# Query features of tiles 4 to 7 transposed as float32, straight from the buffer in which VectorE made them

## The chip, the cores and the metric

The kernel runs on one core of one Trainium2 chip. The metric is device time of one execution in microseconds; the time before is the median of three runs, 615.56 us (614.28 to 615.72). One further execution was recorded by the hardware profiler, and all times of single instructions come from that one.

## The reference

A block works on 2048 tokens of 512 features. The input is normalized; the result is the input plus two branches, a linear attention with learned softmax features and a gated MLP with a mixing over the tokens.

```python
# xn = layernorm(x); result: x + A(xn) + B(xn)
# branch A, 32 heads of 16
pq  = einsum("bhsd,hdf->bhsf", q, w_phi)          # pk in the same way
phi_q = concat([softmax(pq), softmax(-pq)], -1)   # 32 features per head
kv  = einsum("bhsf,bhsd->bhfd", phi_k, v);  z = sum of phi_k over the tokens
o   = (phi_q @ kv) / (phi_q . z + 1e-6);    A = o @ wo
# branch B, 688 channels
z1, z2 = split(gelu(xn @ w_in));  z2 = layernorm(z2)
B = (z1 * (w_sp @ z2 + b_sp)) @ w_out
```

## The kernel before, in words

**Tiles and number forms.** The tokens are 16 tiles of 128. Large products are done in float32r with each operand split into a rounded part h and a rest l: `mm3` (lines 57 to 59) adds ah·bh, ah·bl and al·bh. ScalarE rounds (`round_h`, line 49), VectorE subtracts (`rest_l`, line 53).

**Stages.** First the projections q, k, v and the sums over the keys; then the MLP's input product; then the product with `w_sp` (lines 887 to 930), written as seven products per pair of token tiles; last the stage that the change is in (from line 934): for each pair of tiles i, i+1 it adds up `u @ w_out` (`project_u`, TensorE lines 57 to 59 and 1030), applies `kv` to the query features (`attend`, line 1016), and adds `o @ wo` (`project_o`), whose result goes to `out` by an accumulating DMA on POOL's queue (line 1049).

**Query features.** The exponentials of the queries were stored to DRAM in an early stage (`e_d`). In the last stage `load_q(s, slot("et"))` (line 557) brings tile s back on SP's queue, five tiles ahead. `q_fin` (lines 564 to 571) makes the finished features on VectorE: the product with `zb` into a scratch `tmp` (564), sums and reciprocals (565 to 569), and the scaling in place in `et` (571). `attend` needs them transposed, tokens along the free dimension. There are three ways:
- tiles 0, 1 and 8 to 15 are transposed in blocks of 32 by VectorE (`turn_q`, line 580), put in order by four DMAs to DRAM (`q_d`, line 582), and loaded back (line 958 for tiles 8 to 15);
- tiles 2 and 3 are transposed by TensorE as float32 with `ident` (line 999);
- tiles 4 to 7 are copied by a DMA on POOL's queue from `et` into a float32r tile `er` (line 964) and transposed by TensorE with a float32r identity `ident_r` (line 1001), which ScalarE rounded behind `zb` (line 916).

For a pair, 16 transposes of 128x128 go to four PSUM tiles; ScalarE copies them out (line 1003), and `attend` reads the copies.

**Buffers and order.** `et`, the scratch `tmp`, `zb`, `c` and the weights `wu` share the pool `xz`, 16 buffers of the same size (`slot`). A buffer is free when the last instruction that uses its tile is done; whoever gets it next waits for that. `er` and the tiles `ft` of 8 to 15 come from another pool of three buffers (`er_pair`). The instructions of an engine are put in order by a planner that simulates the program; `tc.issue_after(ins)` orders what a block writes on the engine of `ins` behind `ins`, and only that. `lasts` and `fin` hold such instructions. `lasts[6]` is the last copy into `er`, on POOL; at `i == 2` the load of `z1` for the last gate (line 787, POOL) is put behind it (lines 1103 to 1105).

Of the kernel before, what the change touches and what calls it, by code (L numbers as in the profile page):

```python
# [10 lines left out]
F32 = mybir.dt.float32  # L11
F32R = mybir.dt.float32r
# [6 lines left out]
P = 128  # L19
# [5 lines left out]
NF = 2 * D  # L25
# [16 lines left out]
def mixer(ctx: ExitStack, tc: tile.TileContext, x, x_t, wv, wqkT, phi_bd, wo, w_in, wst, b_r, w_out, out):  # L42
    nc = tc.nc
    pe, act, dve, pool, sp = nc.tensor, nc.scalar, nc.vector, nc.gpsimd, nc.sync


    def round_h(eng, h, src):
        if eng is act:
            return act.activation(h, src, AF.Copy).ins  # L49
        return eng.tensor_copy(h, src).ins  # L50
# [21 lines left out]
    def xz_tile(n, dt, name):  # L72
        return xz.tile([P, SL], dt, tag="xz", name=name)[:, :n]
# [12 lines left out]
    ident = cst.tile([P, P], F32, name="ident")  # L86
# [17 lines left out]
    def group(e, j):  # L104

        return e[:, j * P:(j + 1) * P]
# [88 lines left out]
    with ExitStack() as p0:  # L195
# [154 lines left out]
        def proj_k(s):  # L350
            er = (spare[s] or stage("er")).rearrange("p a b -> p (a b)")[:, :NF + 2 * H] if s in spare else None
            return softmax_pair(wk, proj(s, wqk_h[:, 1], wqk_l[:, 1]), "k", r_x[:, s:s + 1], er=er)
# [69 lines left out]
        def turned(s):  # L422
            pt, i = transposed(s)
            keep(pe=i)
            return pt
# [15 lines left out]
        for cs, pt in zip(halves, pts):  # L441
            src = pt.rearrange("p a b -> p (a b)")
# [11 lines left out]
        pt = turned(1)  # L454
# [26 lines left out]
        pt = turned(2)  # L481
# [24 lines left out]
        for s in range(NT):  # L506
# [6 lines left out]
            er = ek[s] if s < len(ek) else proj_k(s)  # L513
# [42 lines left out]
    def load_q(s, et):  # L556
        sp.dma_start(et[:, :NF + 2 * H], e_d[s])
        return et

    def q_fin(et, tmp, zb):  # L560

        e, r, t, w = et[:, :NF], *(et[:, NF + k * 2 * H:NF + (k + 1) * 2 * H] for k in range(3))
        den = et[:, NF + 6 * H:QW]
        dve.tensor_tensor(tmp, e, zb, op=ALU.mult)
        dve.tensor_reduce(t, heads(tmp), axis=AX.X, op=ALU.add)
        dve.tensor_tensor(t, t, r, op=ALU.mult)
        dve.scalar_tensor_tensor(den, pairs(t, 0), EPS_DEN, pairs(t, 1), op0=ALU.add, op1=ALU.add)
        dve.reciprocal(den, den)
        dve.tensor_tensor(w.rearrange("p (h a) -> p h a", a=2), r.rearrange("p (h a) -> p h a", a=2),
                          den.unsqueeze(2).to_broadcast([P, H, 2]), op=ALU.mult)  # L570
        return e, dve.tensor_tensor(heads(e), heads(e), bc(w, 2 * H), op=ALU.mult).ins
# [25 lines left out]
    def load_a(n):  # L597
        i, q = SEQ[n]
        f = []
        for k in range(2):  # L600
            t = ws.tile([P, QC, P], F32, tag=f"f{k}", bufs=2, name="wf")
            sp.dma_start(t, wst[2 * i + k, :, q * QC:(q + 1) * QC, :])
            f.append(t.rearrange("p (k two) t -> p two k t", two=2))
        return f
# [27 lines left out]
    with ExitStack() as p1:  # L632
        tmp1 = p1.enter_context(left("tmp1", 1))
        kvT = tmp1.tile([P, D], F32, name="kvT")
        zb = tmp1.tile([P, NF], F32, name="zb")
# [41 lines left out]
        for s in range(NE):  # L677
            et = load_q(s, tb.tile([P, QW], F32, name="et") if s else tmp1.tile([P, 4, D], F32, tag="zhl", name="et").rearrange("p a b -> p (a b)")[:, :QW])
            tmp = zw.tile([P, 4, FC], F32, tag="z2", bufs=2, name="qtmp").rearrange("p a b -> p (a b)")[:, :NF]
            e, _ = q_fin(et, tmp, zb)  # L680
# [57 lines left out]
    for s in range(NT):  # L738
# [8 lines left out]
        for k, q in p:  # L747
            ins = act.activation(z[(slice(None), *k)], q, AF.Gelu_apprx_tanh, scale=r_x[:, s:s + 1]).ins
# [35 lines left out]
    def load_z1(i):  # L784
        t = gt.tile([P, 2, FH + REM], F32, tag="z1", name="z1t")
        for k in range(2):
            pool.dma_start(t[:, k, :FH], z1_d[2 * i + k])  # L787
        return t

    def products(n, g):  # L790
        i, q = SEQ[n]
        ops = A.pop(n)
        for name, an, bn in FORM:
            if n % NQ == 0:
                g[name] = psg.tile([P, D], F32, tag="g", name="g")
            dst = g[name][:, :FC]
            for k in range(2):
                (ah, al), (bh, bl) = ops[an], B[2 * q + k][bn]
                mm3(dst, (ah[:, k], al[:, k]), (bh, bl), n % NQ == 0 and k == 0, n % NQ == NQ - 1 and k == 1)
# [44 lines left out]
    def slot(name, dt=F32):  # L844
        return xz_tile(2 * FH, dt, name)
# [22 lines left out]
    def first_gate(i):  # L868
        n = KF * P
        a, b = xz_tile(2 * n, F32R, "u_uh"), xz_tile(n + P, F32R, "ul_rt")  # L870
        u = load_u(i, a[:, :n].bitcast(F32), b[:2 * REM, n:n + P])
        return split_u(*u, k_tiles(a[:, n:2 * n]), k_tiles(b[:, :n]))

    lasts, wu = [None] * 9, []
# [8 lines left out]
            load_w(w_out, rows, h, l, t[c // 2][:, c % 2 * D:(c % 2 + 1) * D])  # L883
            wu.append((h, l))

    g, es, ets, ft, ep, brought = {}, {}, {}, {}, {}, {}
    for n in range(NC):
        i = SEQ[n][0]
        if n % NQ == 1 and i < NP - 1:
            z = load_z1(i)  # L890
        products(n, g)
        if n % NQ == NQ - 1 and i < NP - 1:
            c = gt.tile([P, 2, FU], F32, tag="c", name="c")
            cq = c[:, :, :FH].rearrange("p k (j f) -> p k j f", j=2)
            cb = drain(i, g, cq)
            g = {}
        if n + 3 < NC:
            raw[n + 3] = load_a(n + 3)
        if n + 2 < NC:
            A[n + 2] = prep_a(n + 2, raw.pop(n + 2))  # L900
        if n % NQ == NQ - 1 and i < NP - 1:
            turn = gate(i, cb, z, c, z, prep_a.last)
            if i < NP - 2:
                turn()
            if i in (2, 4):
                s = i // 2 - 1
                e, t = (gt.tile([P, 2, FU], F32, tag=tag, name=name).rearrange("p k f -> p (k f)")[:, :NF]
                        for tag, name in (("c", "c"), ("z1", "z1t")))
                pool.dma_start(e, e_d[s, :, :NF])
                turn_q(s, t, e, pool)  # L910
        if n == NC - 4:
            stage_w()
        if n == NC - 3:
            zs = slot("zb", F32R)
            zb, ident_r = zs[:, :NF].bitcast(F32), zs[:, NF:NF + P]
            round_h(act, ident_r, ident)
            sp.dma_start(zb, zb_d)
            uT = [first_gate(0)]
            ets[2] = load_q(2, slot("et"))
            es[2], last = q_fin(ets.pop(2), slot("qtmp")[:, :NF], zb)  # L920
        if n == NC - 2:
            fq = [slot("f")[:, :NF].rearrange("p (k b c t) -> p k b c t", k=2, c=NB // 2, t=BL) for h in range(2)]
            for k in range(2):
                for h in range(2):
                    sp.dma_start(fq[h][:, k], q_d[k].rearrange("p (b h w) -> h p b w", h=2, w=QB // 2)[h])
            t = xz_tile((KF + 1) * P, F32R, "u1")
            us = {1: load_u(1, t[:, :KF * P].bitcast(F32), t[:2 * REM, KF * P:(KF + 1) * P])}
# [8 lines left out]
    cw = ctx.enter_context(left("cw", 1))  # L936
# [5 lines left out]
                      cw.tile([2 * REM, P], F32R, tag="rt", bufs=6, name="rt"))  # L942

    def er_pair(name):
        return cw.tile([P, 2, NF], F32R, tag="er", bufs=3, name=name)

    def features(s):
        with tc.issue_after(fin[-1]):
            tmp = slot("qtmp")[:, :NF]
            es[s], ins = q_fin(ets.pop(s), tmp, zb)  # L950
        fin.append(ins)
        if s == 3:
            return
        if s >= TQ:
            if s % 2 == 0:
                ft[s] = er_pair("f").bitcast(F32)
            turn_q(s, tmp, es.pop(s), pool)
            brought[s] = sp.dma_start(ft[s - s % 2][:, s % 2], q_d[s]).ins
            return
        e = es[s]  # L960
        if s % 2 == 0:
            ep[s] = er_pair("er")
        es[s] = ep[s - s % 2][:, s % 2]
        lasts[6] = pool.dma_start(es[s].bitcast(F32), e).ins

    def gated(u):
        return split_u(*u, wk.tile([P, KF, P], F32R, tag="uh", name="uh"), wk.tile([P, KF, P], F32R, tag="ul", name="ul"))
# [16 lines left out]
    def attend_T(s):  # L984

        if not s:
            t = [f.rearrange("p k b c t -> p (k b) c t") for f in fq]
            return [t[g // 2][:, :, g % 2 * 2:g % 2 * 2 + 2].rearrange("p b c t -> p c b t") for g in range(NG)]
        if s in ft:
            t = ft[s].rearrange("p k (b c t) -> p (k b) c t", c=NF // P, t=BL)  # L990
            return [t[:, :, 2 * g:2 * g + 2].rearrange("p b c t -> p c b t") for g in range(NG)]
        fs = []
        for g in range(NG):
            pt = pst.tile([P, 2, 2, P], F32, tag="tr", name="ptq")
            for a in range(2):
                for k in range(2):
                    src = group(es[s + k], 2 * g + a)
                    if src.dtype == F32:
                        pe.transpose(pt[:, a, k], src, ident)
                    else:  # L1000
                        pe.transpose(pt[:, a, k].bitcast(F32R), src, ident_r)
            f = wk.tile([P, 2, 2 * P], F32, tag="f", bufs=NG + 1, name="f")
            lasts[5] = act.activation(f, pt.rearrange("p a k b -> p a (k b)"), AF.Copy).ins
            fs.append(f)
        return fs
# [140 lines left out]
```

## Time and profile before

| | us |
|---|---|
| median of three runs (lowest, highest) | 615.56 (614.28, 615.72) |
| the profiled execution, its own time | 615.49 |
| its span in the profile | 613.7 |
| TensorE busy (share) | 606.0 (99%) |
| VectorE busy (share) | 518.8 (85%) |
| ScalarE busy (share) | 261.1 (43%) |
| POOL busy (share) | 134.7 (22%) |

Times in the trace are counted from the start of the span. PE is TensorE's matmul side and PEld its weight load, DVE is VectorE, ACT ScalarE, POOL GpSimd, SP the engine that only issues DMAs. A group is named by its line, its engine, the tile that it writes and the tiles that it reads. Matmuls are pipelined, so the distance from one start to the next tells what a group takes, and not the durations. A wait in brackets names what ended it. The last stage runs from about 480 us to the end.

### The profile page before, as it was taken

Reading aid. Unit: us, or ns where it says so; the run is one execution under the profiler, and the core shown is the slowest. Engines: PE = TensorE matmul, PEld = TensorE weight load, DVE = VectorE, ACT = ScalarE, POOL = GpSimd, SP = SyncE. Lnnn points to the kernel's source line nnn. Section 1 sums busy time; section 2 is a strip of 40 time slices with the busy share of each in tenths; the row PEclk is TensorE's granted clock in tenths of the full one; section 3 lists DMA queues with packets and bytes.
Section 4 is the critical chain, followed back from the end, with each engine's and each line's share of the span. In section 5 each row is a group of like instructions: output and inputs, shape, how many; then the busy total and the mean of one; then the engine's idle time right before and its main releaser. Section 6 shows DMA issues by size and latency. Waiting matters only on the chain.

```text
span 613.7 us, 11396 instructions
## 1 busy us (share of the span) xinstructions
PE 606.0 (99%) x4286; PEld 551.0 (90%) x4286; DVE 518.8 (85%) x929; ACT 261.1 (43%) x416; POOL 134.7 (22%) x236
## 2 busy tenths in 40 slices
PE   8999999999999999999999999999999999999996
PEld 6888888888888999999999999999999977777775
DVE  5999999999988578899889897877879999999921
ACT  4653324423433547887434443342345343332221
POOL 4122232333111014552000002000100042243520
PEclk9999999999999999999999999999999999999999
DMA  9557876566537849001454646455566799898882
GB/s 310 195 128 178 219 173 186 150 161 171 137 113 210 273 159 321 5 1 35 149 128 141 186 97 184 135 156 148 166 172 206 230 342 328 280 278 238 204 212 59
DMA packets 58414, 109.95 MB, mean 179 GB/s; under 512 B 12456, under 2 KB 24616, under 8 KB 58120
## 3 DMA queue, kind: packets, MB, share of 16 engines
q1 hardware_dynamic: 43400, 64.96, 34.9%
q0 software_dynamic: 12656, 38.64, 24.9%
q10 hardware_dynamic: 2304, 5.64, 2.4%
q8 instruction: 33, 0.54, 0.4%
q14 instruction: 21, 0.17, 0.1%
HBM read 66.85 MB, written 35.80 MB: 167 GB/s over the span
## 4 chain that ended last, share of the span: by engine, by line
PE 85%; DVE 6%; DMA 5%; issue 2%; SPq 1%; ACT 1%; POOL 0%; ACTq 0%; DVEq 0%; POOLq 0%
PE g L57 9%; PE g L58 9%; PE g L59 9%; PE proj L57 7%; PE proj L58 7%; PE proj L59 7%; PE zps L58 6%; PE zps L57 6%; PE zps L59 6%; PE pout L57 4%; PE pout L59 4%; PE pout L58 4%; DMA zacc<-e 1%; PE kvps L373 1%; PE po L1016 1%
## 5 line engine op out<-in xcount | busy, mean ns | idle before, releaser
L57 PE MATMUL g<-B,A 128*128 128x344 f32 x448 | 142.5, 319 | 0.4 <-DVE c L810 0.4
L58 PE MATMUL g<-B,A 128*128 128x344 f32 x448 | 142.3, 319 | 0.0
L59 PE MATMUL g<-B,A 128*128 128x344 f32 x448 | 138.9, 318 | 0.0
L57 PEld LDWEIGHTS g<-B,A 128*128 128x128 f32 x448 | 84.0, 188 | 1.0 <-DVE c L810 0.7
L58 PEld LDWEIGHTS g<-B,A 128*128 128x128 f32 x448 | 84.0, 188 | 0.0
L59 PEld LDWEIGHTS g<-B,A 128*128 128x128 f32 x448 | 83.6, 188 | 0.0
L49 ACT ACTIVATE A<-S 128x512 fp32r<-128x512 f32 x64 | 39.3, 628 | 71.2 <-DVE S L622 47.1
L57 PE MATMUL proj<-wqk_h,xT 128*128 128x512 f32 x128 | 50.1, 391 | 0.0
L59 PE MATMUL proj<-wqk_h,xT 128*128 128x512 f32 x128 | 49.8, 389 | 0.0
L58 PE MATMUL proj<-wqk_l,xT 128*128 128x512 f32 x128 | 49.8, 389 | 0.0
L125 ACT ACTIVATE e<-e,r_x 128x1024 f32<-128x1024 f32 x26 | 29.8, 1149 | 42.3 <-DVE e L124 41.3
L53 DVE TENSOR_TENSOR A<-S,A 128x512 fp32r<-128x512 f32 x64 | 43.0, 687 | 3.0 <-ACT A L49 2.8
L49 ACT ACTIVATE A<-wf 128x512 fp32r<-128x512 f32 (+1 forms) x64 | 32.8, 515 | 27.4 <-DMA wf<-in_wst 17.5
L57 PE MATMUL zps<-w1h,xT 128*128 128x344 f32 (+2 forms) x128 | 40.8, 320 | 0.0
L58 PE MATMUL zps<-w1l,xT 128*128 128x344 f32 (+2 forms) x128 | 40.7, 318 | 0.0
L59 PE MATMUL zps<-w1h,xT 128*128 128x344 f32 (+2 forms) x128 | 40.7, 318 | 0.0
L57 PE MATMUL zps<-w2h,xT 128*128 128x344 f32 (+2 forms) x128 | 40.7, 318 | 0.0
L58 PE MATMUL zps<-w2l,xT 128*128 128x344 f32 (+2 forms) x128 | 40.6, 317 | 0.0
L59 PE MATMUL zps<-w2h,xT 128*128 128x344 f32 (+2 forms) x128 | 40.3, 317 | 0.0
L53 DVE TENSOR_TENSOR A<-wf,A 128x512 fp32r<-128x512 f32 (+1 forms) x64 | 35.1, 553 | 3.9 <-ACT A L49 3.7
L128 DVE TENSOR_REDUCE sm<-e 128x64 f32<-128x1024 f32 x26 | 31.1, 1200 | 2.5 <-ACT e L125 2.5
L787 POOL DMA_DIRECT2D z1t<-z_d x16 | 8.7, 552 | 108.3 <-DMA wf<-in_wst 71.0
(222 smaller groups left out, 1437.4 us busy)
## 6 DMA issues: line engine op xcount, KB each, us to landing
wf<-in_wst SPq DMA_DIRECT2D x64, 256.0 KB, 3.4
e_d<-e POOLq DMA_DIRECT2D x16, 544.0 KB, 4.6
et<-e_d SPq DMA_DIRECT2D x16, 544.0 KB, 7.2
z_d<-z1f ACTq DMA_DIRECT2D x16, 344.0 KB, 3.1
z1t<-z_d POOLq DMA_DIRECT2D x16, 344.0 KB, 4.8
zacc<-e POOLq DMA_DIRECT2D x10, 512.0 KB, 4.8
u<-u_d SPq DMA_DIRECT2D x15, 320.0 KB, 5.8
xt<-in_x SPq DMA_DIRECT2D x16, 256.0 KB, 4.0
```

The source lines that it names most:

```text
L49: return act.activation(h, src, AF.Copy).ins
L53: return (eng or dve).tensor_tensor(l, src, h.bitcast(F32), op=ALU.subtract).ins
L57: pe.matmul(dst, ah, bh, start=start, stop=False)
L58: pe.matmul(dst, ah, bl, start=False, stop=False)
L59: return pe.matmul(dst, al, bh, start=False, stop=stop).ins
L125: softmax_pair.last = less, act.activation(e, e, AF.Exp, scale=scale).ins
L128: dve.tensor_reduce(sm, heads(e), axis=AX.X, op=ALU.add)
L373: i = pe.matmul(kv_acc[k:k + QP, m // 4], vs[:, m * QP:(m + 1) * QP], e[:, m * HP:(m + 1) * HP], start=first and m < 4 and len(ready) == n ...
L787: pool.dma_start(t[:, k, :FH], z1_d[2 * i + k])
L1016: lasts[3] = pe.matmul(po[r][c * QP:(c + 1) * QP, k], kvT[rows, m // 2, cols], fs[m // 4][rows, m // 2 % 2], start=True, stop=True).ins
```

## The change

The float32r copies of tiles 4 to 7 are gone: no `er` pair is taken for them and no DMA copies them. `features` returns after `q_fin`, and `attend_T` transposes all of tiles 2 to 7 from `et` as float32 with `ident`. The buffers in `et` are thus in use until TensorE has read them. The float32r identity and its rounding are gone, so `zb` is a plain float32 buffer. `lasts[6]` becomes the last VectorE instruction of `q_fin` (line 571) for the tiles 3 to 7. `er_pair` keeps its size and its three buffers and serves tiles 8 to 15 alone.

```diff
-    g, es, ets, ft, ep, brought = {}, {}, {}, {}, {}, {}
+    g, es, ets, ft, brought = {}, {}, {}, {}, {}
...
         if n == NC - 3:
-            zs = slot("zb", F32R)
-            zb, ident_r = zs[:, :NF].bitcast(F32), zs[:, NF:NF + P]
-            round_h(act, ident_r, ident)
+            zb = slot("zb")[:, :NF]
             sp.dma_start(zb, zb_d)
...
     def er_pair(name):
-        return cw.tile([P, 2, NF], F32R, tag="er", bufs=3, name=name)
+        return cw.tile([P, 2, NF], F32, tag="er", bufs=3, name=name)
 
     def features(s):
         with tc.issue_after(fin[-1]):
             tmp = slot("qtmp")[:, :NF]
             es[s], ins = q_fin(ets.pop(s), tmp, zb)
         fin.append(ins)
-        if s == 3:
-            return
         if s >= TQ:
             if s % 2 == 0:
-                ft[s] = er_pair("f").bitcast(F32)
+                ft[s] = er_pair("f")
             turn_q(s, tmp, es.pop(s), pool)
             brought[s] = sp.dma_start(ft[s - s % 2][:, s % 2], q_d[s]).ins
             return
-        e = es[s]
-        if s % 2 == 0:
-            ep[s] = er_pair("er")
-        es[s] = ep[s - s % 2][:, s % 2]
-        lasts[6] = pool.dma_start(es[s].bitcast(F32), e).ins
+        lasts[6] = ins
...
-                    src = group(es[s + k], 2 * g + a)
-                    if src.dtype == F32:
-                        pe.transpose(pt[:, a, k], src, ident)
-                    else:
-                        pe.transpose(pt[:, a, k].bitcast(F32R), src, ident_r)
+                    pe.transpose(pt[:, a, k], group(es[s + k], 2 * g + a), ident)
```

## The prediction

> **What bounds the kernel now.** I read the page first: span, busy shares, the slices and the chain that ended last.
>
> ```profile
> span 613.7 us, 11396 instructions
> ...
> PE 606.0 (99%) x4286; PEld 551.0 (90%) x4286; DVE 518.8 (85%) x929; ACT 261.1 (43%) x416; POOL 134.7 (22%) x236
> ...
> PE   8999999999999999999999999999999999999996
> ...
> PE 85%; DVE 6%; DMA 5%; issue 2%; SPq 1%; ACT 1%; POOL 0%; ACTq 0%; DVEq 0%; POOLq 0%
> ```
>
> TensorE is busy for 606.0 of 613.7 us and carries 85% of the chain. A saving elsewhere counts only where TensorE waits for it. So the next view is what TensorE waited for, from 20 us before the first instruction that the change touches (455 us) to the end:
>
> ```profile
> engine line waited for: us in total, times, longest us
> PE g L57 <- DVE c L810: 0.4, 1, 0.4
> PE ptq L1001 <- DMA er<-et: 0.2, 1, 0.2
> ```
>
> There are two waits in 159 us, and only one belongs to the code that changes: a transpose of L1001 waits 0.2 us for a copy `er<-et`. That is nearly all there is to win. What can be lost is TensorE time in the transposes themselves, and cover on the engines that feed it. The timeline of TensorE around the three groups of transposes (pairs 2/3, 4/5, 6/7) gives the prices; the columns are start, duration, and in brackets the idle time before it:
>
> ```profile
> 501.80 0.39 PE L59 MATMUL pout<-woh,oT 128*128 128x512 f32 x1
> 502.04 1.91 PE L999 MATMUL ptq<-ident,et 128*128 128x128 f32 x16
> 503.70 0.48 PE L57 MATMUL pout<-wu,uh 128*128 128x512 f32 x1
> ...
> 518.04 0.39 PE L59 MATMUL pout<-woh,oT 128*128 128x512 f32 x1
> 518.27 0.46 PE L1001 MATMUL ptq<-zb,er 128*128 128x128 f32 x4
> 518.97 1.23 PE L1001 MATMUL ptq<-zb,er 128*128 128x128 f32 x12 [0.24 <-DMA er<-et]
> 520.04 0.47 PE L57 MATMUL pout<-wu,uh 128*128 128x512 f32 x1
> ...
> 534.40 0.39 PE L59 MATMUL pout<-woh,oT 128*128 128x512 f32 x1
> 534.63 1.49 PE L1001 MATMUL ptq<-zb,er 128*128 128x128 f32 x16
> 535.96 0.47 PE L57 MATMUL pout<-wu,uh 128*128 128x512 f32 x1
> ```
>
> The kernel already holds both forms. Pair 2/3 goes the float32 way (L999), and its 16 transposes hold TensorE from 502.04 to 503.70, 1.66 us or 104 ns each. Pair 6/7 goes the float32r way with nothing to wait for: 534.63 to 535.96, 1.33 us or 83 ns each. Pair 4/5 takes 518.27 to 520.04, 1.77 us, which is the same work with the copy's wait in it (1.77 - 1.33 = 0.44 us lost, of which the bracket shows 0.24 as idle).
>
> **The change, part by part.** *Transposes.* 32 of them go from float32r to float32. Pair 4/5: from 1.77 to 1.66 us, since the wait goes too, -0.11. Pair 6/7: from 1.33 to 1.66, +0.33. TensorE is the path that sets the end, so the sum is +0.22 us. Bounds: if float32 cost no more than float32r, 2 x 1.33 against 1.77 + 1.33 is -0.44; if each transpose passed through the array four times, it would be spaced like a matmul of 512 columns, 0.23 us (518.04 to 518.27), 16 x 0.23 = 3.68 us a pair, +4.26. I take 1.66 because that row is the same operation on the same kind of tile.
>
> The weight loads of the two forms look alike:
>
> ```profile
> L999 PEld LDWEIGHTS ptq<-ident,et x16: 138/140/143, 501.8 to 503.6; 128*128 128x128 f32 x16
> L999 PE MATMUL ptq<-ident,et x16: 270/273/273, 502.0 to 503.7; 128*128 128x128 f32 x16
> ...
> L1001 PEld LDWEIGHTS ptq<-zb,er x32: 138/142/143, 518.0 to 535.8; 128*128 128x128 f32 x32
> ```
>
> The Trainium skill ("TensorE: Matmul & The Clock Gate", Weight-path perf modes) speaks against this change: fast weight load is on for 128 weights only when their type is not FP32. By its price for a plain load, columns over 1.2, a float32 transpose would cost 107 ns, 16 of them 1.71 us (an estimate from that page), and the sum would be +0.32 instead of +0.22. That a float32 group is slower agrees with the trace (104 against 83 ns); that its load is longer doesn't (140 against 142 ns).
>
> *Copies.* Four DMA copies of 512 KB on POOL's queue go, and the one rounding of the identity on ScalarE:
>
> ```profile
> L964 POOL DMA_DIRECT2D er<-et x4: 546/552/559, 506.5 to 523.6; - x4
> ...
> DMA to landing us min/median/max: 5.4/6.7/8.7
> ```
>
> ```profile
> 475.94 0.29 ACT L49 ACTIVATE zb<-ident 128x128 fp32r<-128x128 f32 x1
> ```
>
> Together 2.2 us of POOL and 0.29 us of ScalarE. The waits above name no POOL instruction and no ScalarE one as holding TensorE up, so both count 0 (they can't gain more than the 0.44 already counted). The transposes now wait for VectorE's last product (L571) instead of for the landing. It ends well ahead:
>
> ```profile
> 511.95 1.23 DVE L571 TENSOR_TENSOR et<-et 128x1024 f32<-128x1024 f32 x1
> ...
> 522.13 1.23 DVE L571 TENSOR_TENSOR et<-et 128x1024 f32<-128x1024 f32 x1
> ```
>
> Tile 5 is done at 513.18, 5.1 us before 518.27; tile 7 at 523.36, 11.3 us before 534.63. The copies out of PSUM (L1003) and the matmuls behind a group move together with it: 0.
>
> *Buffers held longer.* A tile's features used to leave their `xz` buffer when the copy had landed; now they stay until TensorE has transposed them. Of 16 buffers, 6 hold output weights, 1 `zb` and 1 `c`; 8 circulate between loaded tiles and the scratch of `q_fin`. Later loads wait longer on SP:
>
> ```profile
> 515.49 3.77 SPq L557 DMA_DIRECT2D et<-e_d  x2
> ...
> 529.75 0.46 SPq L557 DMA_DIRECT2D et<-e_d  x1
> ```
>
> ```profile
> DMA to landing us min/median/max: 5.4/7.4/8.0
> ```
>
> ```profile
> 523.27 1.22 DVE L564 TENSOR_TENSOR qtmp<-et,zb 128x1024 f32<-128x1024 f32 x1
> ...
> 537.09 1.22 DVE L564 TENSOR_TENSOR qtmp<-et,zb 128x1024 f32<-128x1024 f32 x1
> ...
> 554.12 1.22 DVE L564 TENSOR_TENSOR qtmp<-et,zb 128x1024 f32<-128x1024 f32 x1
> ```
>
> The two loads at 515.49 are tiles 10 and 11 (the second is issued at 518.9, when tile 5's copy has landed). At worst both move to 520.04, the end of the transposes of 4/5. With a landing of 8.0 us they are there by 529; tile 10 is wanted at 537.09. Tile 12's load at 529.75 moves to 536 at worst, lands by 544, wanted at 554.12. The `u` loads behind them on SP are four tiles ahead of use. I take 0; without that cover a late tile would cost what it is late, one for one. Around 523 us six tiles (6 to 11) and one scratch are live, seven of eight, so the scratch of tile 8 still finds a buffer.
>
> *A lost order.* `lasts[6]` was a DMA on POOL, and the load of the last `z1` at `i == 2` was put behind it. It is now a VectorE instruction, and an order among the instructions of one engine says nothing to a load on POOL. That load may be issued as early as its buffer is free, after the writes `ur_d<-z1t`:
>
> ```profile
> 493.27 2.25 POOL L839 DMA_DIRECT2D ur_d<-z1t  x4
> ...
> 519.66 1.10 POOL L787 DMA_DIRECT2D z1t<-z_d  x2
> ```
>
> Those are issued by 495.5; with a landing like the copies' median, 6.7 us, the load could start around 502 instead of 519.66. There the DMA engines are full (share and GB/s are the last columns):
>
> ```profile
> 502.00:506.00 4.00, 4.00 (x27) 3.60 (x26) 3.79 (x8) 2.66 (x5) 1.39 (x2) 1.00 1.03 384
> 506.00:510.00 4.00, 4.00 (x45) 2.69 (x45) 3.11 (x4) 1.80 (x3) 0.56 (x1) 1.00 1.09 275
> ```
>
> Its 2 x 344 KB are 2.1 us of that traffic at 330 GB/s (the mean of the two rows), so tile 5's load may be up to 2.1 us later. VectorE can give way there, by these rows:
>
> ```profile
> 507.94 0.83 DVE L53 TENSOR_TENSOR ul<-u,uh 128x640 fp32r<-128x640 f32 x1 [0.86 <-ACT uh L49]
> ...
> 511.16 0.63 DVE L53 TENSOR_TENSOR oT<-po,oT 128x512 fp32r<-128x512 f32 x1
> ```
>
> ```profile
> 512.78 0.39 PE L57 MATMUL pout<-woh,oT 128*128 128x512 f32 x1
> ```
>
> It idles 0.86 us ahead of `ul`, and `oT` is ready at 511.79, 0.99 us before TensorE reads it. So at most 2.1 - 0.86 - 0.99 = 0.25 us would reach TensorE. The lower end is 0 (the load stays late, or tile 5 has landed); a gain has no place, as no wait for `z1` exists. I take 0, because 2 MB of copies leave the same full stretch just behind.
>
> **Sum.** The profiled execution took 615.49 us, its span 613.7 and 1.8 around it: 615.49 + 0.22 = 615.7. It lies 0.07 below the median of the three runs, 615.56, so the sum stands for the median as well. A difference under 0.3% (1.85 us) can't be told from no change here; 0.22 us is a ninth of that.
>
> **The rivals.** *Early `z1` load collides:* the price above, 615.7 + 0.25, at most 617.8 if none of the 2.1 us were hidden. For it speaks the full DMA, against it the two covers on VectorE. 5%.
>
> *Slower, buffers run out:* if one buffer fewer circulates than I count, or they are dealt out in another order, the scratch of tile 8 gets none at 523.27 and waits for the transposes of 6/7, which end at 535.96. It decides from the moment the eighth buffer is missing at 523. Then VectorE, 3.79 us busy of 4 in such stretches, runs its feature chain 12.7 us late. TensorE takes up tiles 8 and 9 at 554.58; tile 9's load back is issued at 546.54 and, sized like the copies, takes 5.4 us at least, so there are 2.6 us of slack:
>
> ```profile
> 546.54 0.32 SPq L958 DMA_DIRECT2D f<-q_d  x1
> ```
>
> ```profile
> 554.58 1.02 PE po L1016 x32
> ```
>
> 12.7 - 2.6 = 10.1 us of stall, 625.8. Against it is my count of seven of eight. 4%.
>
> *Slower, four passes:* float32 through the array four times, +4.26, 619.8. The Trainium skill ("FP8 and Floating Point Precision", TensorE Precision Notes) gives true FP32 four passes. The L999 rows speak against it for transposes: 16 took 1.66 us, not 3.68. 1%.
>
> *Faster by over 0.3%:* the copies' traffic slows something in TensorE's stream that no wait shows, or the tail is ordered better without them. In the stretch where they run, matmuls of 512 columns start 0.23 us apart (518.04 to 518.27), as they do at 534.40 to 534.63, when the last copy has landed. 1.85 us is four times the 0.44 that the copies cost. I give it 4%, around 613.
>
> **Numbers.** No measurable change with 615.7: 86%. Together with the mild form of the first rival (5%, 1 of which beyond the bound) the chance of "within 0.3%" is 0.90; slower 0.06 (1 + 4 + 1); faster 0.04. The runs of before reach from 614.28 to 615.72, so the same spread around 615.7 gives 614.2 to 616.5; up to 617.6 to take in a stall from the early load and an unexpected order on VectorE. The four-pass end and the buffer rival stay outside, with 5%.
>
> **What would show it.** In the changed kernel's timeline two more groups like the one at 502.04, 16 float32 transposes in 1.66 us each and no idle bracket in the first; no wait of TensorE for `er`; VectorE's features at the same places; the load of `z1` somewhere between 502 and 520. The prediction is wrong if a group takes nearer 3.7 us, if TensorE waits for `f`, `oT` or `ptq` between 505 and 560 us, or if VectorE's L564 at 523.27 comes much later.

## The result, and the profile after

| | before | after |
|---|---|---|
| median, us (9 executions each) | 615.72 | 619.54 |
| lowest and highest, us | 614.28, 617.37 | 616.79, 621.12 |
| the profiled execution, us | 615.49 | 619.99 |
| its span in the profile, us | 613.7 | 618.3 |

The ratio of after to before is 1.0051, with a 95% interval of 1.0034 to 1.0068 (the two medians alone give 1.0062). The change makes the kernel slower by half a per cent. Forecast were 615.7 us, with 617.6 as the upper end, and no measurable difference.

The page of the kernel after: its span, the busy times, the granted clock in 40 slices, and the chain by engine.

```profile
span 618.3 us, 11383 instructions
...
PE 608.3 (98%) x4286; PEld 553.2 (89%) x4286; DVE 519.1 (84%) x929; ACT 260.1 (42%) x415; POOL 132.9 (21%) x232
...
PEclk9999999999999999999999999999999979999999
...
PE 91%; DVE 3%; DMA 3%; SPq 1%; issue 1%; ACT 0%; POOL 0%; ACTq 0%; DVEq 0%; POOLq 0%
```

TensorE still sets the end. Its instructions are the same in number, but it is busy for 2.3 us longer, and in one slice, near 500 us, its clock is not full. The next view is what TensorE waited for from 455 us on, in the kernel after (total, times, longest):

```profile
PE pout L57 <- ACT oT L49: 2.7, 1, 2.7
```

The wait for `er` is gone, as is the one for `c`. A single new wait stands there, for `oT`, a tile that the change doesn't touch. TensorE's timeline of the kernel after shows where it is and what follows it (start, duration, idle time before it):

```profile
494.71 0.63 PE L1018 MATMUL pout<-wu,u 96*128 96x512 f32 x2
498.05 0.80 PE L57 MATMUL pout<-woh,oT 128*128 128x512 f32 x1 [2.71 <-ACT oT L49]
498.65 0.63 PE L58 MATMUL pout<-wol,oT 128*128 128x512 f32 x1
499.07 0.63 PE L57 MATMUL pout<-woh,oT 128*128 128x512 f32 x1
...
504.46 0.40 PE L58 MATMUL pout<-wol,oT 128*128 128x512 f32 x1
504.69 0.62 PE L59 MATMUL pout<-woh,oT 128*128 128x512 f32 x2
...
506.51 1.91 PE L989 MATMUL ptq<-ident,et 128*128 128x128 f32 x16
508.18 0.47 PE L57 MATMUL pout<-wu,uh 128*128 128x512 f32 x1
...
522.78 1.91 PE L989 MATMUL ptq<-ident,et 128*128 128x128 f32 x16
524.44 0.48 PE L57 MATMUL pout<-wu,uh 128*128 128x512 f32 x1
...
539.02 1.91 PE L989 MATMUL ptq<-ident,et 128*128 128x128 f32 x16
540.68 0.48 PE L57 MATMUL pout<-wu,uh 128*128 128x512 f32 x1
```

Two things happen before the first group of transposes. TensorE stands idle for 2.71 us, and then its matmuls of 512 columns start 0.42 us apart (498.65 to 499.07) instead of 0.23 us (504.46 to 504.69). The table of stretches of the kernel after gives the clock (the third column from the end; then DMA share and GB/s):

```profile
492.00:496.00 4.00, 3.34 (x15) 2.42 (x13) 0.69 (x1) 0.63 (x1) 1.73 (x4) 1.00 0.97 272
496.00:500.00 4.00, 1.95 (x5) 1.56 (x6) 2.45 (x4) 2.36 (x5) 0.00 (x0) 0.68 1.03 368
500.00:504.00 4.00, 4.00 (x11) 3.13 (x10) 3.79 (x7) 0.72 (x1) 0.00 (x0) 0.50 1.07 322
504.00:508.00 4.00, 4.00 (x25) 3.45 (x25) 3.97 (x5) 1.72 (x4) 1.36 (x2) 0.97 1.02 403
```

If the clock is either full or half, the three rows below 1.00 hold 4 x 0.32 / 0.5 = 2.6, 4.0 and 4 x 0.03 / 0.5 = 0.2 us of half clock, 6.8 us together. It stood at half from about 497.4 to 504.2. The fall comes while TensorE is still idle, as a stretch of 1 us shows:

```profile
497.00:498.00 1.00, 0.00 (x0) 0.00 (x0) 0.45 (x1) 1.00 (x3) 0.00 (x0) 0.71 1.05 390
```

Here 0.29 / 0.5 = 0.58 us are at half clock, so it fell at about 497.42, 0.63 us before TensorE went on at 498.05.

**Where the wait comes from.** `oT` is a copy by ScalarE, and ScalarE was late because of the row ahead of it. First the two kernels' ScalarE and the issue of the output weights (`wof`, line 850, SP's queue, 16 loads of 64 KB). Before:

```profile
481.42 8.15 SPq L850 DMA_DIRECT2D wof<-in_wo  x16
...
491.88 0.63 ACT L49 ACTIVATE woh<-wof 128x512 fp32r<-128x512 f32 x1 [1.94 <-DMA wof<-in_wo]
492.70 1.09 ACT L49 ACTIVATE oT<-po 128x512 fp32r<-128x512 f32 x2 [0.19 <-PE po L1016]
...
DMA to landing us min/median/max: 1.9/2.8/3.8
```

After:

```profile
480.35 12.34 SPq L850 DMA_DIRECT2D wof<-in_wo  x16
...
493.61 0.63 ACT L49 ACTIVATE woh<-wof 128x512 fp32r<-128x512 f32 x1 [4.32 <-DMA wof<-in_wo]
496.89 0.63 ACT L49 ACTIVATE woh<-wof 128x512 fp32r<-128x512 f32 x1 [2.64 <-DMA wof<-in_wo]
497.42 1.06 ACT L49 ACTIVATE oT<-po 128x512 fp32r<-128x512 f32 x2
...
DMA to landing us min/median/max: 3.5/4.6/6.1
```

In ScalarE's order the four roundings `woh` stand ahead of `oT`. Before, the last weight is rounded at 491.88 and `oT` follows at 492.70, over 3 us before TensorE wants it at 496.54. After, SP begins to issue the weights 1.1 us earlier but takes 12.34 us for it instead of 8.15, each lands later (4.6 us instead of 2.8 in the median), the last is rounded at 496.89, and `oT` comes behind it with no gap.

What is new on the DMA engines at this time stands on POOL's timeline of the kernel after:

```profile
479.17 1.06 POOL L787 DMA_DIRECT2D z1t<-z_d  x2 [23.84 <-PE g L59]
489.15 2.35 POOL L837 DMA_DIRECT2D u_d<-z1t  x4 [8.92 <-DVE z1t L833]
491.49 2.24 POOL L839 DMA_DIRECT2D ur_d<-z1t  x4
```

This is the load of the last gate's `z1`, 2 x 344 KB, which before was issued at 519.66. It has lost its order behind `lasts[6]` and goes 40 us earlier, 1.2 us ahead of the first output weight.

**Theory 1:** the early load of `z1` delays the output weights, hence ScalarE and TensorE, and the idle time costs the clock. **Theory 2:** the float32 transposes, or the buffers that they hold longer, move loads and VectorE's work about, and the late weights are a sign of that. **Theory 3**, for the part behind the wait: the low clock comes from something else than the idle time.

### The profile page after: what moved, and what is told of

It reads as the page before. It is cut to its first block, busy times and chain, and to the rows that moved or that the text cites. A ratio compares the mean times of both kernels' runs of the same rounds, so it can differ in the third digit from the quotient of the medians.

```text
span 618.3 us, 11383 instructions
## 1 busy us (share of the span) xinstructions
PE 608.3 (98%) x4286; PEld 553.2 (89%) x4286; DVE 519.1 (84%) x929; ACT 260.1 (42%) x415; POOL 132.9 (21%) x232
## 4 chain that ended last, share of the span: by engine, by line
PE 91%; DVE 3%; DMA 3%; SPq 1%; issue 1%; ACT 0%; POOL 0%; ACTq 0%; DVEq 0%; POOLq 0%
PE g L57 10%; PE g L58 10%; PE g L59 10%; PE proj L58 7%; PE proj L57 7%; PE proj L59 7%; PE zps L59 6%; PE zps L58 6%; PE zps L57 6%; PE pout L57 5%; PE pout L58 5%; PE pout L59 5%; PE po L1004 1%; DMA zacc<-e 1%; DMA kvT<-kvT_d 1%; PE kvps L373 1%
```

## The experiments

Each ratio is to the kernel before as it ran beside the experiment: a median of 616.37 us (34 executions) for the first four, 615.97 us (17) for the last three. Medians of different groups are thus not to be compared to the tenth of a us.

**The early load taken back.** The kernel after, with the load of `z1` put behind the accumulating DMA of tile 3 on POOL.

```diff
-        lasts[6] = ins
...
                 ins = pool.dma_start(out[rows, :], xr, accum_op=ALU.add).ins
+                lasts[6] = ins
```

> The kernel after, with the load of the last z1 again behind a DMA on POOL (the accumulating one of tile 3), so that it starts around 522 us instead of 479. Float32 transposes, held buffers and the missing copies stay. Theory 1 (the early z1 load delays the loads of wo, TensorE waits 2.7 us ahead of project_o(0) and then runs at half clock for 6 us): no wait of TensorE there, clock 1.0 throughout, 615.7 to 616.2 us, ratio to before 1.000. Theory 2 (the float32 transposes or the buffers held longer cost it): 619 to 620, ratio 1.005 to 1.006.

Measured: 615.74 us in the median of 12 executions, ratio to before 0.9987 (0.9969 to 1.0005). The load's row, the weights and `oT` behind them, TensorE at the place of the stall, and the clock there:

```profile
L787 POOL DMA_DIRECT2D z1t<-z_d x2: 887/890/894, 518.6 to 519.1; - x2
```

```profile
480.32 9.76 SPq L850 DMA_DIRECT2D wof<-in_wo  x16
...
491.98 0.63 ACT L49 ACTIVATE woh<-wof 128x512 fp32r<-128x512 f32 x1 [2.40 <-DMA wof<-in_wo]
492.52 1.07 ACT L49 ACTIVATE oT<-po 128x512 fp32r<-128x512 f32 x2
...
DMA to landing us min/median/max: 1.9/2.8/4.4
```

```profile
494.68 0.63 PE L1017 MATMUL pout<-wu,u 96*128 96x512 f32 x2
495.15 0.40 PE L57 MATMUL pout<-woh,oT 128*128 128x512 f32 x1
...
500.64 1.91 PE L988 MATMUL ptq<-ident,et 128*128 128x128 f32 x16
```

```profile
496.00:500.00 4.00, 4.00 (x20) 3.28 (x19) 3.79 (x7) 1.97 (x3) 0.00 (x0) 1.00 1.05 390
```

From 455 us to the end TensorE waits for nothing. All float32 transposes and held buffers are still there, so theory 2 falls. This kernel is also the measure for the loss, since up to the stall it runs like the kernel after (494.68 and 494.71). There the first matmul with `oT` starts at 498.05 instead of 495.15: 2.90 us by the wait. From it to the transposes are 506.51 - 498.05 = 8.46 us instead of 500.64 - 495.15 = 5.49: 2.97 us by the clock. Together 5.87 us; the spans differ by 618.3 - 612.5 = 5.8. Nothing else is needed to explain the two profiles.

**The lost order alone.** The kernel before, with copies and float32r transposes as they were, but the load of `z1` without its order.

```diff
-            with tc.issue_after(lasts[6]):
-                z = load_z1(NP - 1)
+            z = load_z1(NP - 1)
```

> The kernel before, with only the order of the last z1 load taken away; copies by DMA and float32r transposes stay. Theory 1: the wait ahead of project_o(0) and the half clock appear, 618.5 to 620 us, ratio 1.004 to 1.007. Theory 2: 615.7, ratio 1.000.

Measured: 619.12 us (11 executions), ratio 1.0042 (1.0026 to 1.0058), most of the change's 1.0051 and not to be told from it. The load, TensorE's wait and the clock:

```profile
L787 POOL DMA_DIRECT2D z1t<-z_d x2: 536/537/538, 479.7 to 480.2; - x2
```

```profile
498.55 0.50 PE L57 MATMUL pout<-woh,oT 128*128 128x512 f32 x1 [2.48 <-ACT oT L49]
```

```profile
496.00:500.00 4.00, 1.51 (x6) 1.23 (x6) 1.96 (x4) 1.60 (x3) 0.00 (x0) 0.92 0.97 356
500.00:504.00 4.00, 4.00 (x13) 3.12 (x13) 3.79 (x7) 1.48 (x2) 0.00 (x0) 0.65 1.07 353
```

The stall comes with the early load and without one float32 transpose more. So theory 1 is shown from both sides: without the early load the stall goes, and with it alone the stall comes. The half clock is shorter here: 4 x 0.08 / 0.5 + 4 x 0.35 / 0.5 = 3.4 us.

**The float32 transposes alone.** The kernel before, copies kept, with the copied tiles transposed as float32.

```diff
-                    if src.dtype == F32:
-                        pe.transpose(pt[:, a, k], src, ident)
-                    else:
-                        pe.transpose(pt[:, a, k].bitcast(F32R), src, ident_r)
+                    pe.transpose(pt[:, a, k], src if src.dtype == F32 else src.bitcast(F32), ident)
```

> The kernel before, with only the transposes of tiles 4 to 7 made float32 (read from the copies, which stay, as does the late z1 load). Theory 1: two groups of 1.66 us or a little more where the copy is late, plus 0.3 to 0.7 us, 616.0 to 616.4, not told from no change (ratio 1.0005 to 1.001). Theory 2 with the transposes as the cause: 619 to 620, ratio 1.005.

Measured: 616.11 us (12 executions), ratio 0.9994 (0.998 to 1.0008). The first of the two groups on TensorE's timeline:

```profile
517.82 1.94 PE L998 MATMUL ptq<-ident,er 128*128 128x128 f32 x16
519.51 0.48 PE L57 MATMUL pout<-wu,uh 128*128 128x512 f32 x1
```

It takes 1.69 us, the second group 1.67 (534.11 to 535.78), and in the whole there is no difference that can be told from none. The transposes are not the cause.

**Half of the load early.** The kernel after, with one of the two 344 KB pieces of `z1` left early (480.0 us) and the other late (520.5 us).

```diff
         for k in range(2):
-            pool.dma_start(t[:, k, :FH], z1_d[2 * i + k])
+            with tc.issue_after(lasts[6]) if i == NP - 1 and k else ExitStack():
+                pool.dma_start(t[:, k, :FH], z1_d[2 * i + k])
...
-        lasts[6] = ins
...
                 ins = pool.dma_start(out[rows, :], xr, accum_op=ALU.add).ins
+                lasts[6] = ins
...
-            with tc.issue_after(lasts[6]):
-                z = load_z1(NP - 1)
+            z = load_z1(NP - 1)
```

> The kernel after, with only one of the two halves of the z1 load early (344 KB at about 479 us), the other behind the accumulating DMA of tile 3. Theory 1 with the bytes as the cause: the last piece of wo comes 2 to 2.5 us later than in the kernel before instead of 5, so TensorE waits 0 to 1 us ahead of project_o(0) and the clock stays up, 616 to 617 us, ratio 1.000 to 1.002. If not the bytes but one transfer ahead of wo is enough: 619. Theory 2: 619 to 620.

Measured: 616.82 us (12 executions), ratio 1.0004 (0.9981 to 1.0028). The last weight, and TensorE's stall at the same place:

```profile
495.57 0.63 ACT L49 ACTIVATE woh<-wof 128x512 fp32r<-128x512 f32 x1 [3.70 <-DMA wof<-in_wo]
...
496.74 0.50 PE L57 MATMUL pout<-woh,oT 128*128 128x512 f32 x1 [0.52 <-ACT oT L49]
```

```profile
500.00:504.00 4.00, 3.99 (x26) 3.27 (x25) 3.83 (x8) 2.37 (x5) 1.52 (x2) 1.00 1.06 322
```

Half of the bytes leave 0.52 us of the 2.71, and the clock of this execution stays full. The delay of the weights themselves falls by less: the last is rounded 495.57 - 491.98 = 3.6 us later than in the first experiment, where all the bytes make it 4.9. (Against the kernel before it is 3.7, and 2 to 2.5 were expected: a miss.) The wait is short because the cover ahead of `oT`, 2.0 us in the first experiment, takes its part, and because TensorE comes to the place at 496.22 instead of 495.15. The order that the planner gave VectorE and SP differs here from the kernel after, so the dose is shown only roughly. One of the 12 executions took 621.68 us at a mean clock of 0.993; no trace shows where.

**The kernel after once more, unchanged,** beside the next two.

> The kernel after, unchanged, beside the next two on one chip. Theory 1 and theory 2 both: ratio to before 1.003 to 1.007.

Measured: 618.45 us (12 executions), ratio 1.0033 (1.001 to 1.0056). Its profiled execution:

```profile
497.60 0.76 PE L57 MATMUL pout<-woh,oT 128*128 128x512 f32 x1 [2.00 <-ACT oT L49]
```

```profile
496.00:500.00 4.00, 2.40 (x6) 1.92 (x7) 2.90 (x4) 1.83 (x4) 0.00 (x0) 0.71 0.98 337
500.00:504.00 4.00, 4.00 (x17) 3.26 (x16) 3.79 (x8) 1.84 (x3) 0.00 (x0) 0.86 1.08 340
```

The wait is 2.00 us instead of 2.71, and the half clock is 4 x 0.29 / 0.5 + 4 x 0.14 / 0.5 = 3.4 us instead of 6.8. The stall belongs to the kernel, its size changes from one execution to the next, and with it the number of spells of half clock. The first profile of after caught much of the low clock: its mean, 0.993, is the lowest of its nine executions. In the 12 here the mean granted clock is 0.9971, beside 0.9982 in the 17 of the kernel before; over 617 us that is an estimated 0.7 us, where the mean times differ by 2.1. So on average the clock makes the smaller part of the loss. Two of the 21 executions of after, of 621.12 and 620.50 us, even show a mean clock of 1.000; what they lost, no trace here shows.

**The idle time filled.** The kernel after, with ten matmuls on the identity between `project_u` of tile 1 and the first `project_o`; nothing reads their result. (The trace counts each as two.) This separates theory 3: without idle time the clock should stay full.

```diff
+        if not i:
+            idle = pst.tile([P, ND, P], F32, tag="tr", name="idle")
+            with tc.issue_after(lasts[2]):
+                for k in range(FILL):
+                    fill = pe.matmul(idle[:, k % ND], ident, ident, start=True, stop=True, skip_group_check=True).ins
...
-            project_o(i + k, oT, p.pop(i + k))
+            with tc.issue_after(fill):
+                project_o(i + k, oT, p.pop(i + k))
```

> The kernel after, early z1 load and all, with ten matmuls on the identity (128 columns of float32, 0.2 to 0.25 us each, results not used) put on TensorE between project_u(1) and project_o(0), into the wait. They make 2 to 2.5 of the 2.7 us busy and add nothing to what project_o waits for. If the half clock comes from the idle time: the wait shrinks to 0.2 to 0.7 us, the clock stays 1.0, the 3 us that 15 slow matmuls cost are back, ratio 1.000 to 1.002, below the kernel after by 0.003 to 0.005. If the clock falls for another reason, such as the DMA load of that stretch: half clock as before, ratio 1.005 to 1.006.

Measured, at the place itself:

```profile
496.13 2.39 PE L1085 MATMUL idle<-ident 128*128 128x128 f32 x20
498.79 0.50 PE L57 MATMUL pout<-woh,oT 128*128 128x512 f32 x1 [0.27 <-ACT oT L49]
```

```profile
500.00:504.00 4.00, 4.00 (x19) 3.32 (x18) 3.79 (x8) 2.08 (x3) 0.88 (x1) 1.00 1.07 351
```

`oT` is as late as in the kernel after, but the clock stays full, and the first transposes start at 504.75, 1.76 us earlier than in the profile of after, though the first matmul with `oT` starts 0.74 us later. Theory 3 falls. The expectation for the whole time was missed: 623.87 us (6 executions), ratio 1.0116 (1.0087 to 1.0146). TensorE now waits further on for VectorE, whose work stands in another order there, in a part that doesn't bear on the question:

```profile
PE pout L59 <- DVE oT L53: 3.7, 2, 2.2
```

**Tiles 6 and 7 without TensorE.** The first experiment's kernel with `TQ = 6`, so that VectorE and DMAs turn tiles 6 and 7 too: two groups of transposes instead of three.

```diff
-    TQ = 8
+    TQ = 6
```

> The kernel with the late z1 load (e1), with tiles 6 and 7 transposed by VectorE as tiles 8 to 15 are (TQ = 6). TensorE loses one group of transposes, 1.66 us. VectorE gains two transposes of 1.24 us, each with a round trip through DRAM. If the features of tiles 8 and 9 have the 2.6 us of slack that I worked out: about 614, ratio 0.996 to 0.998. If VectorE's chain is too tight there: TensorE waits for f ahead of tiles 6 to 9, ratio 1.000 to 1.005.

Measured: 629.32 us (6 executions), ratio 1.0211 (1.0176 to 1.0245). TensorE's waits:

```profile
PE po L1003 <- DMA f<-q_d: 7.3, 2, 5.2
```

The 1.66 us saved on TensorE are lost several times over. It waits 2.06 us for the turned features of tiles 6 and 7 and 5.21 us for those of tiles 10 and 11, and 3.4 and 6.8 us at half clock come with these waits; the span is 624.4 us, 11.9 more than the first experiment's. That is worse than the worst that was expected, 1.005: VectorE's chain of features has no room for two more tiles. So the transposes on TensorE pay for themselves, as float32 too.

None of the kernels beats the kernel before beyond what the measurement can tell. The first experiment's, with neither copies nor early load, is the nearest to it, at 0.9987 (0.9969 to 1.0005).

## Why the prediction was wrong, step by step

- *Transposes:* right. All three groups take 1.66 to 1.67 us; the third experiment has 1.69 for the first on its own. The sum of +0.22 shows in the profiles: after is 506.51 - 502.04 = 4.47 us behind before at the first group and 540.68 - 535.96 = 4.72 behind past the third. By the estimate from the Trainium skill ("TensorE: Matmul & The Clock Gate", LDWEIGHTS) it would have been 1.71 a group; the trace decides for 1.66.
- *Copies:* right as far as it can be told. Kept (third experiment, 0.9994) or gone (first, 0.9987), the intervals overlap for the most part.
- *Buffers held longer:* right. With all three groups float32, the kernel after and the first experiment have no wait of TensorE for `f`, `ptq` or a tile's features behind 500 us.
- *A lost order:* this step failed. It saw that the load loses its order, but took its buffer to be the one that `ur_d<-z1t` reads. The load of the last gate takes its tile from a pool of its own (`gt` is bound anew at line 935 of the kernel before), which is free once the matmuls `g` are done; on POOL's row at 479.17 the trace names one of them, line 59, as what ended the wait. So it went at 479, not at 502; it met the output weights, not the load of tile 5; and the cover that was counted, VectorE's 0.86 and 0.99 us, stands at another place. The row that gave this away was in reach: on POOL's timeline of before, the engine sits idle for 34.6 us ahead of 490.94. Without its order the load went into this hole, at 479 to 480 us in every profile of a kernel that lets it.
- *The size of the delay,* within the same step: 2.1 us of traffic was the most allowed. Measured between the first experiment and after, the last weight is rounded 496.89 - 491.98 = 4.9 us later for the same 688 KB. Priced by bytes alone, even the right place would have come out at almost nothing, since the cover there is 495.15 - (492.52 + 0.59) = 2.0 us, of the first experiment's rows (0.59 is the first of the two copies). Of the 4.9 us, 3.5 are there when SP issues the last load (492.2 instead of 488.7), and the rest is its landing. Between the 16 loads SP waits, by the trace, until loads that it issued just before them have landed: 1.4 us for `u<-ur_d` and 1.9 us for `kvT<-kvT_d` in the kernel after, 1.1 us for `u<-u_d` and 0.7 us for `kvT<-kvT_d` in the first experiment. So the early load slows the small loads twice, in their landing and by SP's waits for others. Why SP waits for those, the runs don't show.
- *A term that was not there:* the clock. The sum had a wait cost what it lasts. In the profile of after 2.90 us of wait brought 2.97 us more; in the second profile of after and with the lost order alone, the way from the first matmul with `oT` to the transposes is 7.16 and 7.18 us instead of 5.49, 1.7 us more.
- *A small slip:* 0.22 us is an eighth of 1.85, not a ninth; nothing hangs on it.
- *The start:* at 490 us the profile of after is 1.36 us ahead of before (`po` at 490.15 against 491.51), which is why 5.87 us of loss make 4.6 us of span. The second experiment, whose order up to there is that of before, passes the place at 490.87, so part of this lies between executions; the rest isn't settled.

Of the rivals, the early `z1` load was the right mechanism at the wrong place: 5%, with 615.95 and at most 617.8, where 619.54 was measured. Four passes, at 619.8, came nearest in time and are wrong by every group in the trace. Buffers running out and the faster case didn't show. The list of what would prove the prediction wrong named a wait for `oT`, but from 505 us on; it came at 498. The error in the chances is that all of "within 0.3%" hung on one buffer's identity, read from the order of the trace and not from the code.

## What to carry to other kernels

When an edit replaces the instruction that another one is ordered behind, ask on which engine the new one is: on another engine the order is gone, and the ordered DMA can move forward to where its buffer comes free, found from the pool in the code and from the hole in its queue's timeline. Price it there, against the loads that are under way with it and against what stands behind the first instruction that waits for them, and not by its bytes alone. On TensorE, where it paces the kernel, a wait of two microseconds or more can cost up to twice its length: in these profiles 1.7 to 3.0 us lost at half clock came on top of 2.0 to 2.9 us of wait.

## What the runs showed of the hardware

**Half clock in spells of 3.4 us.** Idle times of TensorE of 2.00 us (the second profile of after), 2.48 us (lost order alone) and 2.71 us (the first profile of after) came with 3.4, 3.4 and 6.8 us at half clock; 0.52 us (half of the load) came with none. The other waits of these runs fit in: 2.06 us (tiles 6 and 7 without TensorE) and 2.17 us (idle time filled, further on) came with 3.4 us each, 5.21 us (tiles 6 and 7 without TensorE, further on) with 6.8, 1.52 us (idle time filled) with none. Twice 3.4 is 6.8, so it looks as if the clock were set for one spell at a time. The Trainium skill ("TensorE: Matmul & The Clock Gate", What's actually happening) states a free-running window of 3413 ns, after whose idleness the clock is halved; the length of the spells agrees. Its rule that gaps should not go beyond about 3 us (section "Why this matters for your kernels") is too lenient by these runs: 2.00 us was enough. One spell or two goes with where the clock fell. By stretches of 1 us, in the four cases with one spell it fell 0.08 to 1.10 us after TensorE had gone on; in the two with two spells it fell while TensorE was still idle, 0.63 us (2.71 us of idle time) and 1.58 us (5.21) before the end. So it looks as if a spell that begins in idle time is followed by another; six cases don't make it a rule, and no experiment moved the idle time against the spells.

**A load on POOL's queue delays small loads on SP's queue by more than its share of traffic.** 688 KB, issued 1.2 us ahead, brought the median landing of 64 KB loads from 2.8 us (the first experiment) to 4.6 and their issue on SP from 9.76 to 12.34 us for 16, and the last was rounded 4.9 us later, where the bytes are 2.1 us at 330 GB/s. With the lost order alone the landing goes from 2.8 us (before) to 4.1 and the issue from 8.15 to 12.41 us.
